# An attention scan in front of two expert layers: late rows of chunk 0 loaded batch by batch, chunk 1's rows loaded by ScalarE's queue, first pieces in another order

## The chip, the cores and the metric

The kernel runs on one core of a Trainium2 chip. The core has TensorE (PE) for matmuls, VectorE (DVE), ScalarE (ACT) and GpSimd (POOL) for elementwise work, and SyncE (SP), which here only issues DMA transfers. The core's 16 DMA engines move data between HBM and the on-chip memory. The metric is the device time of one launch in microseconds, lower is better.

## The reference

What is computed, cut to what matters (the state is carried over 768 positions; batch 4, 8 heads, head size 32, state size 16):

```python
# attention: x, a, B, C in; per batch and head
log_a = np.log(np.clip(a, 1e-06, 1.0)); cum = np.cumsum(la, axis=-1)      # per chunk
L = np.exp(cum[..., :, None] - cum[..., None, :]) * causal
y = (np.einsum('bhin,bhjn->bhij', Cc, Bc) * L) @ xc + (Cc @ state) * np.exp(cum)[..., None]
state = decay_full * state + sum_j Bc_j xc_j decay_from_j
# 4 x 768 tokens of 256 go through two layers of width 2048
h = x @ w_in; x = (h * (1 / (1 + np.exp(-1.702 * h)))) @ w_out
h = x @ w_in2; out = (h * np.clip(h + 3.0, 0.0, 6.0) / 6.0) @ w_out2
```

## The kernel before

**The scan.** The 768 positions are cut into eight chunks of 96. A piece q is one batch of one chunk, q = 4 x chunk + batch. For a piece, score matmuls (`s_mm`, L624) give C times B, which VectorE multiplies by the decay (`g_mul`, L627), or ScalarE copies and GpSimd multiplies (`g_copy` L630, `g_pool` L634); `y_mm` (L650), called by `visit`, multiplies that by x and the state; `y_state` (L664) takes the state back, and casts (L684) and differences (L693, L696) make of the output the two float parts, `bx_0h` and `bx_0l`, that the layers read. Chunk 0 has a path of its own: scores per half of its rows (`sx_mm` L539, `sy_mm` L548), products (`gx_mul` L552, `gx_copy` L555, `gx_pool` L558, `gy_mul` L561), and `yx_mm` (L573) for two pieces at a time. Pieces 4 and 5 are the first two of chunk 1. Later pieces are visited in pairs, or one by one where the pair stands in `SOLO`.

**The layers.** The trunk starts with units of 12 wide matmuls: `l1` (L852) and `l2` (L878). Later blocks go by a Strassen scheme (L1018). A weight tile is loaded (`w_load` L368), scaled by ScalarE (`w_scale` L372), split into a low part (`w_low`, L380 on ScalarE, L382 on VectorE), joined (`w_join` L386 on VectorE, into `dec`), and cast to a high part `wh` (`w_top` L389) whose rest is `wl` (`w_bottom` L393). The tiles are `bx_w0`, `bx_w1` and so on.

**What sets the order.** The class `Schedule` sorts what `add` recorded: each step has an engine, an estimated duration, a key (a due time), and the names it reads and writes; the tables at the top of the file (`TOPV`, `GMX`, `KX`, `KV`, `PK`, `WAFTER` and so on) set keys and engines. The engines then run their instructions in this order. At most eight DMA loads are outstanding over all queues: each waits for the landing of the one eight before it. Before the change, ScalarE's queue carries only four of the eight loads of chunk 0's B and C rows (`in_bcz`, L604) and two constant tables; all else goes by SyncE: x0 (`x0_load`, L531 for the first 64 rows of chunk 0, L528 for the late rows 64 to 95), the four loads of chunk 1's B and C rows (`in_bc0`, `r16_load`, L601, 16 x 1792 each), the store of the clipped decays (L470), the weight tiles, and chunk 1's x values (`x_load`, L592).

Of the kernel before, what the change touches and what calls it, by code (L numbers as in the profile page):

```python
# [71 lines left out]
DECODE = (13.3, 7.5)  # L72


GMX = (0, 1, 3)
KX = (1.1, 4.5, 4.5)
KV = (5.9, 9.7, 10.5)
# [184 lines left out]
def ssd_moe_kernel(ctx: ExitStack, tc: tile.TileContext, xs, aa, bc, bcz_d, bc0, wu, pat, idn, out):  # L262
# [453 lines left out]
    for i in range(2):  # L716
        add("SP", (1.2, 0.6)[i], -40 + i, x0_load, i, r=["xs:0"], w=[f"xs:0.{i}"], kb=(262, 131)[i])
    for q in range(NC * NB):
        c, b = divmod(q, NB)
# [17 lines left out]
        if q < NB and b % 2 == 0:  # L737
# [14 lines left out]
            if p == 0:  # L752
# [420 lines left out]
```

## Time and profile before

| | before |
|---|---|
| time, median of 3 runs | 568.96 us (568.78 to 569.59) |
| profiled execution, its own time | 569.68 us |
| its span | 567.9 us, granted clock 0.999 |
| TensorE busy | 555.0 us, 98% |
| VectorE, ScalarE, GpSimd busy | 431.3, 327.2, 297.4 us |
| HBM read, written | 33.87 MB, 3.26 MB |

The page gives the busy time of each engine first, then the span in 40 slices of 14.2 us with a digit for the busy tenths. The timeline lists instructions of one engine in order of their start; a bracket at a row's end names the idle time before it and what ended it. Rows of consecutive instructions of one kind are drawn together, with the time from the first start to the last end; the last of them ends in a pipeline, so that the next row can start before.

### The profile page before, as it was taken

Reading aid. Unit: us, or ns where it says so; the run is one execution under the profiler, and the core shown is the slowest. Engines: PE = TensorE matmul, PEld = TensorE weight load, DVE = VectorE, ACT = ScalarE, POOL = GpSimd, SP = SyncE. Lnnn points to the kernel's source line nnn. Section 1 sums busy time; section 2 is a strip of 40 time slices with the busy share of each in tenths; the row PEclk is TensorE's granted clock in tenths of the full one; section 3 lists DMA queues with packets and bytes.
Section 4 is the critical chain, followed back from the end, with each engine's and each line's share of the span. In section 5 each row is a group of like instructions: output and inputs, shape, how many; then the busy total and the mean of one; then the engine's idle time right before and its main releaser. Section 6 shows DMA issues by size and latency. Waiting matters only on the chain.

```text
span 567.9 us, 9146 instructions
## 1 busy us (share of the span) xinstructions
PE 555.0 (98%) x3392; PEld 449.6 (79%) x3392; DVE 431.3 (76%) x630; ACT 327.2 (58%) x604; POOL 297.4 (52%) x281
## 2 busy tenths in 40 slices
PE   7699999999999999999999999999999999999996
PEld 6477778878788788788888888888888888888885
DVE  6649997569688886578757888777877876887875
ACT  2477645344434436686868777566554575555543
POOL 4277488687643105457899786777231385101000
PEclk9999999999999999999999999999999999999999
DMA  8995323034224200430103310000200000200002
GB/s 140 315 261 182 119 92 84 1 115 115 83 90 138 87 1 1 162 107 30 38 1 112 111 39 0 1 1 2 74 2 0 1 0 2 74 2 0 1 0 75
DMA packets 22160, 37.73 MB, mean 66 GB/s; under 512 B 10548, under 2 KB 14372, under 8 KB 22116
## 3 DMA queue, kind: packets, MB, share of 16 engines
q1 hardware_dynamic: 20836, 36.47, 21.7%
q10 hardware_dynamic: 1280, 0.68, 0.5%
q8 instruction: 27, 0.44, 0.3%
q14 instruction: 17, 0.14, 0.1%
HBM read 33.87 MB, written 3.26 MB: 65 GB/s over the span
## 4 chain that ended last, share of the span: by engine, by line
PE 93%; DVE 2%; POOL 2%; issue 1%; ACT 1%; DMA 0%; ACTq 0%; POOLq 0%
PE acc L878 45%; PE h L1018 19%; PE h L852 15%; PE s L1018 4%; PE y L1018 4%; PE s L624 2%; PE h L650 1%; POOL wl L393 1%; PE acc L573 1%; POOL gl L868 0%; PE acc L494 0%; PE s L650 0%; DMA pat_sb<-in_pat 0%; PE acc L580 0%; DVE ov_a L700 0%
## 5 line engine op out<-in xcount | busy, mean ns | idle before, releaser
L868 POOL TENSOR_TENSOR gl<-gg,gh 128x512 fp32r<-128x512 f32 x56 | 81.0, 1446 | 156.1 <-PE h L1018 72.9
L878 PE MATMUL acc<-gh,wl 128*128 128x512 f32 x256 | 100.5, 392 | 0.0
L878 PE MATMUL acc<-gh,wh 128*128 128x512 f32 x256 | 99.9, 390 | 0.0
L878 PE MATMUL acc<-gl,wh 128*128 128x512 f32 x256 | 80.3, 390 | 0.0
L878 PE MATMUL acc<-ov_b,wh 128*128 128x512 f32 x256 | 78.9, 389 | 0.0
L1030 DVE TENSOR_TENSOR ov_b<-h,ov_b 128x512 f32<-128x512 f32 x64 | 44.1, 689 | 40.9 <-PE h L1018 39.3
L589 DVE TENSOR_TENSOR_SCAN ov_a<-ov_a,pat_sb 112x448 f32<-112x448 f32 x52 | 67.3, 1329 | 1.1 <-DMA ov_a<-acl_d 1.1
L865 ACT CAST gh<-gg 128x512 fp32r<-128x512 f32 x80 | 49.7, 621 | 20.2 <-DVE gg L862 18.7
L878 PEld LDWEIGHTS acc<-gh,wl 128*128 128x128 f32 x256 | 48.1, 188 | 10.7 <-issue 0.2
L393 POOL TENSOR_TENSOR wl<-dec,wh 128x512 fp32r<-128x512 f32 x32 | 46.0, 1439 | 19.4 <-ACT wh L389 13.4
L878 PEld LDWEIGHTS acc<-gl,wh 128*128 128x128 f32 x256 | 48.1, 188 | 10.2
L878 PEld LDWEIGHTS acc<-ov_b,wh 128*128 128x128 f32 x256 | 48.1, 188 | 10.0
L878 PEld LDWEIGHTS acc<-gh,wh 128*128 128x128 f32 x256 | 48.1, 188 | 9.9
L859 ACT ACTIVATE gg<-h 128x512 f32<-128x512 f32 x48 | 28.7, 598 | 43.5 <-PE h L1018 35.6
L868 DVE TENSOR_TENSOR gl<-h,gh 128x512 fp32r<-128x512 f32 x47 | 32.1, 683 | 27.1 <-ACT gh L865 26.9
L878 PE MATMUL acc<-ov_b,wl 128*128 128x512 f32 x128 | 49.8, 389 | 0.0
L856 ACT ACTIVATE gg<-h 128x512 f32<-128x512 f32 x39 | 23.3, 598 | 44.4 <-PE h L852 43.8
L856 ACT ACTIVATE h<-h 128x512 f32<-128x512 f32 x39 | 22.7, 582 | 44.8 <-PE h L852 35.2
L868 POOL TENSOR_TENSOR ov_b<-ov_b 128x512 fp32r<-128x512 f32 x24 | 31.6, 1315 | 25.4 <-ACT ov_b L865 22.3
L865 ACT CAST gh<-h 128x512 fp32r<-128x512 f32 x47 | 27.6, 586 | 7.8 <-DVE h L862 5.7
L1030 DVE TENSOR_TENSOR h<-h,ov_b 128x512 f32<-128x512 f32 x32 | 22.4, 699 | 8.7 <-PE h L1018 8.4
L862 DVE SCALAR_TENSOR_TENSOR gg<-gg,h 128x512 f32<-128x512 f32 x40 | 27.1, 678 | 1.5 <-ACT gg L859 1.2
(295 smaller groups left out, 1305.3 us busy)
## 6 DMA issues: line engine op xcount, KB each, us to landing
bx_w<-in_wu SPq DMA_DIRECT2D x32, 512.0 KB, 5.6
ov_a<-acl_d SPq DMA_DIRECT2D x26, 392.0 KB, 3.7
ov_a<-in_xs SPq DMA_DIRECT2D x7, 384.0 KB, 4.4
ov_a<-in_bc SPq DMA_DIRECT2D x96, 24.0 KB, 2.5
out<-gg SPq DMA_DIRECT2D x6, 192.0 KB, 1.9
out<-gg SPq DMA_DIRECT2D x4, 128.0 KB, 1.8
ov_a<-in_bc SPq DMA_DIRECT2D x4, 112.0 KB, 9.1
ov_a<-in_xs SPq DMA_DIRECT2D x3, 128.0 KB, 3.7
```

Source lines behind the costliest of these rows:

```text
L393: e.tensor_tensor(out=lo, in0=B_(f"dec:{p}").bitcast(F32), in1=hi.bitcast(F32), op=ALU.subtract)
L589: nc.vector.tensor_tensor_scan(t, a, pat_sb, 0.0, ALU.mult, ALU.add)
L624: nc.tensor.matmul(out=s_bank(q, g)[:, k, :], lhsT=t[r:r + NS, 0, i], rhs=t[r:r + NS, 1, i], start=True, stop=True)
L852: nc.tensor.matmul(out=B_(hn(u)), lhsT=w[:, 128 * j:128 * j + 128], rhs=x[:, j], start=low in (None, 1) and i + j == 0, stop=low == 2 and ...
L856: nc.scalar.activation(B_(dst), B_(src), AF.Gelu_apprx_sigmoid)
L859: nc.scalar.activation(B_(dst), B_(src), AF.Relu, bias=3.0)
L862: nc.vector.scalar_tensor_tensor(out=B_(dst), in0=B_(g), scalar=6.0, in1=B_(h), op0=ALU.min, op1=ALU.mult)
L865: nc.scalar.copy(B_(dst), B_(src))
L868: e.tensor_tensor(out=B_(dst), in0=B_(src), in1=B_(hi).bitcast(F32), op=ALU.subtract)
L878: nc.tensor.matmul(out=B_(acc[d]), lhsT=w[:, 256 + 128 * d:384 + 128 * d], rhs=g, start=first and d not in seen, stop=last and d not in [v ...
L1018: nc.tensor.matmul(out=B_(dst), lhsT=w, rhs=x, start=start and i == 0, stop=i == 2, skip_group_check=True)
L1030: nc.vector.tensor_tensor(out=B_(dst), in0=B_(a), in1=B_(b), op=ALU.add)
```

## The change

Three things change around the start, and with them the tables that set the order.

1. The late rows of chunk 0 are four loads of 32 x 256, one for each batch, on ScalarE's queue; it was one load of 128 x 1 x 256 on SyncE's.
2. The four loads of chunk 1's rows go by ScalarE's queue, with a key of their own (`R1K`); they stood on SyncE's, ahead of the decays' store and the weights.
3. On TensorE the second `yx_mm` stands ahead of the scores of pieces 4 and 5. One product of chunk 0 moves from ScalarE and GpSimd to VectorE (`GMX`). Pair 3 is visited piece by piece too (`SOLO`). Nine tops on VectorE become five (`TOPV`), the rest goes to ScalarE; other tables and the planner's durations and DMA model are set anew.

The names of lines move by 6 up to some line 590 of before, by 7 in the layers (L368 is L374, L624 is L630, L852 is L859).

```diff
-TOPV = (3, 5, 6, 7, 8, 9, 10, 12, 14)
+TOPV = (2, 5, 8, 9, 10)
...
-GMX = (0, 1, 3)
-KX = (1.1, 4.5, 4.5)
-KV = (5.9, 9.7, 10.5)
+GMX = (0, 1)
+KX = (2.7, 4.2, 4.7)
+KV = (10.1, 6.3, 11.5)
...
-SOLO = (5,)
+SOLO = (3, 5)
 solo = lambda q: q < 4 or q // 2 in SOLO
-R16 = 10.0
+R16 = 4.0
+RQ = ("ACT", "ACT", "ACT", "ACT")
+X0Q = ("SP", "ACT")
+R1K = -23.0
+PXK = -96
+X0K = (-51.7, -38.4)
...
-WAFTER = (2.7, 4.2, 4.0, 6.5, 14.0, 7.1, 19.7)
+WAFTER = (4.3, 4.5, 3.9, 6.1, 12.0, 7.6, 21.3)
...
-                pipe = max(pipe, t + 1.3) + o["kb"] / 240.0
-                end = pipe + 0.8
+                pipe = max(pipe, t + 1.2) + o["kb"] / 390.0
+                end = pipe + 0.5
...
-    def x0_load(i):
-        if i:
-            nc.sync.dma_start(out=B_("xs:0")[:, 2], in_=xs[0][64:CH].rearrange("j b f -> b j f"))
-        else:
-            for j in range(2):
-                nc.sync.dma_start(out=B_("xs:0")[64 * j:64 * j + 64, 0:2], in_=xs[0][0:64].rearrange("j (p b) f -> j b p f", b=2)[:, j])
+    def x0_load(eng, i):
+        if i > 1:
+            b = i - 2
+            eng.dma_start(out=B_("xs:0")[32 * b:32 * b + 32, 2], in_=xs[0][64:CH, b])
+        else:
+            eng.dma_start(out=B_("xs:0")[64 * i:64 * i + 64, 0:2], in_=xs[0][0:64].rearrange("j (p b) f -> j b p f", b=2)[:, i])
...
-    for i in range(2):
-        add("SP", (1.2, 0.6)[i], -40 + i, x0_load, i, r=["xs:0"], w=[f"xs:0.{i}"], kb=(262, 131)[i])
+    for i in range(2 + NB):
+        e = X0Q[i > 1]
+        add(e, 0.4 if i > 1 else 0.6, X0K[i > 1] + i, x0_load, DQ[e], i, r=["xs:0"], w=[f"xs:0.{i}"], kb=80 if i > 1 else 250)
...
-                    e = "SP" if c or s else "ACT"
+                    e = ("SP" if s else "ACT") if c == 0 else RQ[i] if c == 1 else "SP"
                     n = f"rows.{c}.{i}.{s}"
-                    add(e, 0.84 if c > 1 else 0.42 if c else 0.66, t - R16 + 1 if c else -70 + i, r16_load, {"SP": nc.sync, "ACT": nc.scalar}[e], c, i, s,
-                        r=[rn], w=[n], kb=140 if c == 1 else 80, after=(0.0, 3.0, 16.0, 16.0)[min(c, 3)])
+                    add(e, 0.84 if c > 1 else 0.43 if c else 0.66, t - R16 + 1 if c > 1 else R1K + i if c else -70 + i, r16_load, DQ[e], c, i, s,
+                        r=[rn], w=[n], kb=(200, 390)[c] if c < 2 else 80, after=(0.0, 3.0, 16.0, 16.0)[min(c, 3)])
```

SyncE's order from x0 to the third weight tile before (`ov3_a` holds the x rows, `ov2_a` the B and C rows, `acl_d` the stored decays):

```order
L531 DMA ov3_a_121<-in_xs 64x2x256 x2
L528 DMA ov3_a_121<-in_xs 128x1x256
L601 DMA ov2_a_120<-in_bc0 16x1792 x4
L470 DMA acl_d_126<-gg0_107 128x224
L368 DMA bx_w0_205<-in_wu 128x1024
L368 DMA bx_w1_207<-in_wu 128x1024
L592 DMA ov3_a_121<-in_xs 96x1024
L368 DMA bx_w2_227<-in_wu 128x1024
```

And the same stretch of SyncE now:

```order
L537 DMA ov3_a_121<-in_xs 64x2x256 x2
L476 DMA acl_d_126<-gg0_107 128x224
L374 DMA bx_w0_180<-in_wu 128x1024
L374 DMA bx_w1_185<-in_wu 128x1024
L598 DMA ov3_a_121<-in_xs 96x1024
L374 DMA bx_w2_230<-in_wu 128x1024
```

The late rows and the four row loads of chunk 1 are gone from it, and the tiles follow x0 directly.

ScalarE's order ahead of chunk 0's state before (`h0`, `h1`, `y0` are score banks, `ov4_a` holds products):

```order
L604 DMA ov2_a_120<-in_bcz 16x8x112 x2
L555 COPY ov4_a_122<-h0_127 128x448
L555 COPY ov4_a_122<-h1_128 128x448
L372 ACTIVATE bx_w0_205<-bx_w0_205 128x512
L555 COPY ov4_a_122<-y0_134 128x448
L666 COPY st_sb_117<-acc3_132 128x2x16
```

And now:

```order
L535 DMA ov3_a_121<-in_xs 32x256 x4
L607 DMA ov2_a_120<-in_bc0 16x1792
L561 COPY ov4_a_122<-h0_127 128x448
L561 COPY ov4_a_122<-h1_128 128x448
L378 ACTIVATE bx_w0_180<-bx_w0_180 128x512
L607 DMA ov2_a_120<-in_bc0 16x1792 x3
L378 ACTIVATE bx_w1_185<-bx_w1_185 128x512
L378 ACTIVATE bx_w2_230<-bx_w2_230 128x512
L378 ACTIVATE bx_w3_253<-bx_w3_253 128x512
L672 COPY st_sb_117<-acc3_132 128x2x16
```

Three of the row loads stand behind the scaling of tile 0, and tiles 1 to 3 are scaled ahead of chunk 0's state; the third copy of a score bank is gone.

ScalarE's order at the opening of the trunk before (`acc` is a bank of outputs, the last cast writes what the first wide matmul reads):

```order
L684 CAST bx_0h_352<-acc2_131 128x2x96
L372 ACTIVATE bx_w2_227<-bx_w2_227 128x512
L389 CAST wh0_71<-dec0_103 128x512
L372 ACTIVATE bx_w3_284<-bx_w3_284 128x512
L664 COPY st_sb_117<-acc3_132 128x2x2x16
L684 CAST bx_0h_352<-acc3_132 128x2x96
```

And now:

```order
L378 ACTIVATE bx_w4_298<-bx_w4_298 128x512
L636 COPY ov4_a_122<-s0_133 112x448
L386 ACTIVATE s0_133<-bx_w0_180 128x512
L378 ACTIVATE bx_w5_337<-bx_w5_337 128x512
L395 CAST wh0_71<-dec0_103 128x512
L378 ACTIVATE bx_w6_412<-bx_w6_412 128x512
L670 COPY st_sb_117<-acc3_132 128x2x2x16
L690 CAST bx_0h_375<-acc3_132 128x2x96
```

Tiles 4, 5 and 6 are scaled here, where it was tiles 2 and 3.

## Rows read from the trace of the kernel before

**Rows 1.** The page's first part: busy time, share of the span, instructions.

```profile
PE 555.0 (98%) x3392; PEld 449.6 (79%) x3392; DVE 431.3 (76%) x630; ACT 327.2 (58%) x604; POOL 297.4 (52%) x281
```

**Rows 2.** Waits of TensorE: what waited, for what, total, times, longest (us).

```profile
PE acc L573 <- issue: 2.7, 1, 2.7
...
PE h L852 <- ACT bx_0h L684: 1.3, 1, 1.3
```

**Rows 3.** Timeline of TensorE: start, length, instruction, idle time before it.

```profile
15.56 0.62 PE L573 MATMUL acc<-ov_a 64*32 64x112 f32 x16
...
20.07 0.38 PE L573 MATMUL acc<-sf,ov_a 32*32 32x48 f32 x5 [2.67 <-issue]
20.37 0.53 PE L624 MATMUL h<-ov_a 16*112 16x112 f32 x2
...
22.30 0.62 PE L573 MATMUL acc<-ov_a 64*32 64x112 f32 x16
...
28.88 1.22 PE L852 MATMUL h<-bx_0h,wh 128*128 128x512 f32 x2 [1.31 <-ACT bx_0h L684]
```

**Rows 4.** Timeline of SyncE's DMA queue: when its loads were issued.

```profile
6.26 1.84 SPq L601 DMA_DIRECT2D ov_a<-in_bc  x4
...
8.61 0.93 SPq L368 DMA_DIRECT2D bx_w<-in_wu  x2
13.51 0.33 SPq L592 DMA_DIRECT2D ov_a<-in_xs  x1
```

**Rows 5.** Waits of SyncE's queue up to 46 us.

```profile
SPq L592 <- DMA ov_a<-in_xs: 4.0, 1, 4.0
```

**Rows 6.** Timeline of ScalarE: the first scaling of a weight tile.

```profile
18.70 0.66 ACT L372 ACTIVATE bx_w<-bx_w 128x512 f32<-128x512 f32 x1 [6.52 <-DMA bx_w<-in_wu]
```

**Rows 7.** Windows: length, busy of PE, PEld, DVE, ACT, POOL; clock, DMA share, GB/s.

```profile
0.00:9.00 9.00, 5.96 (x25) 4.57 (x26) 5.17 (x10) 2.00 (x3) 4.74 (x17) 1.00 0.78 139
9.00:17.00 8.00, 8.00 (x184) 5.82 (x183) 6.87 (x10) 0.97 (x2) 2.22 (x2) 1.00 0.99 141
17.00:22.00 5.00, 2.33 (x56) 2.02 (x48) 0.66 (x1) 2.55 (x9) 1.59 (x2) 1.00 1.03 292
22.00:25.00 3.00, 3.00 (x79) 1.59 (x73) 2.55 (x7) 0.99 (x5) 0.68 (x2) 1.00 1.03 410
```

**Rows 8.** DMA between 8.5 and 11.5, 13 and 16, 17.6 and 21.6 us.

```profile
DMA packets 173, 0.28 MB, mean 94 GB/s; under 512 B 36, under 2 KB 149, under 8 KB 173
...
DMA packets 129, 0.37 MB, mean 122 GB/s; under 512 B 25, under 2 KB 51, under 8 KB 129
...
DMA packets 299, 1.07 MB, mean 268 GB/s; under 512 B 37, under 2 KB 37, under 8 KB 299
```

**Rows 9.** DMA between 6.0 and 6.5 us by queue: packets, MB, share.

```profile
q1 hardware_dynamic: 84, 0.08, 110.9%
q10 hardware_dynamic: 5, 0.00, 4.8%
```

**Rows 10.** DMA between 17.5 and 18.6 us, the instruction queue.

```profile
q8 instruction: 1, 0.02, 6.2%
```

**Rows 11.** Timelines of VectorE (three rows) and ScalarE (one) ahead of the trunk.

```profile
22.29 0.62 DVE L627 TENSOR_TENSOR ov_a<-h,ov_a 112x448 f32<-112x448 f32 x1 [4.63 <-ACT gg L690]
22.83 0.62 DVE L627 TENSOR_TENSOR ov_a<-s,ov_a 112x448 f32<-112x448 f32 x1
...
26.49 0.68 DVE L386 SCALAR_TENSOR_TENSOR dec<-bx_w,s 128x512 uint32<-128x512 uint32 x1
...
27.73 0.67 ACT L372 ACTIVATE bx_w<-bx_w 128x512 f32<-128x512 f32 x1
```

**Rows 12.** Timeline of TensorE: a pair visited at once, and half a pair.

```profile
60.85 0.97 PE L650 MATMUL s<-ov_a 112*32 112x112 f32 x32
...
80.95 0.59 PE L650 MATMUL y<-ov_a 112*32 112x112 f32 x16
```

**Rows 13.** The page's second part: VectorE's busy tenths in 40 slices.

```profile
DVE  6649997569688886578757888777877876887875
```

More of the change, by code (lines that the diff above doesn't have):

```diff
@@ L44 @@
 LP = 9
-DL = (3.8, 1.0, 0.2, 2.7, 0.6)
-TOPV = (3, 5, 6, 7, 8, 9, 10, 12, 14)
+DL = (3.9, 1.2, -0.4, 2.5, 1.0)
+TOPV = (2, 5, 8, 9, 10)
 TOPP = (2, 3, 7, 24, 27, 28)
@@ L49 @@
 BOT = lambda p: "POOL"
-LOWD = (0, 1, 2, 16, 17, 21)
+LOWD = (1, 2, 3, 11, 16, 17, 21)
 LOW = lambda p: "DVE" if p in LOWD else "ACT"
-GMS = (0, 2, 3, 4, 6, 7, 9, 22)
+GMS = (0, 2, 3, 4, 7, 10, 20, 22)
 GMP = lambda q, g: 2 * q + g in GMS if q < 12 else g == 1 and q > GM1
 GM1 = 32
-GL0 = (1, 2, 9, 13)
+GL0 = (1, 2, 9)
 GLP = lambda kind, k, m: m % 4 in GLM[k] if k else m in GL0
-GLM = ((0,), (0, 1, 2), (0, 1, 2), (0,))
+GLM = ((2, 3), (0, 1), (0, 1, 3), (0,))
 TE = lambda kind, v: "DVE" if kind == "A" and v[0] == "T" else "POOL"
@@ L71 @@
 PKEY = (0.7, 0.7, 1.4, 3.4, 4.1, 6.1, 6.8)
[L72 to L77 removed]
+DECODE = (13.3, 7.6)
+GMX = (0, 1)
+KX = (2.7, 4.2, 4.7)
+KV = (10.1, 6.3, 11.5)
 def SBANK(q, g):
@@ L101, in YBANK @@
     return f"{'ys'[q % 2]}:y{q}" if solo(q) else f"{'ys'[q // 2 % 2]}:y{q // 2 * 2}"
-P0 = (4.6, 7.5)
-YP = (0, 4)
-PK = (45.0, 4.0, 94.9, 4.3, 116.4, 5.8, 149.3, 3.9)
+P0 = (5.6, 7.7)
+YP = (1, 4)
+PK = (45.0, 4.0, 93.9, 4.3, 117.0, 5.5, 148.3, 4.2)
 UGAP = (16, 0.25)
@@ L706, in ssd_moe_kernel @@
     add("DVE", 0.38, -80, a_clip, w=["gg:acl"])
-    add("DVE", 0.26, -80, a_part, 0, r=["gg:acl"], w=["gh:acl"])
-    add("DVE", 0.30, -80, a_part, 1, r=["gg:acl", "gh:acl"], w=["al"])
+    add("DVE", 0.57, -80, a_part, 0, r=["gg:acl"], w=["gh:acl"])
+    add("DVE", 0.57, -80, a_part, 1, r=["gg:acl", "gh:acl"], w=["al"])
     add("SP", 0.4, -1, a_store, r=["gg:acl"], w=["acl_d"], kb=115)
     add("POOL", 0.15, -84, ay_zero, new=["gl:acl"])
-    add("DVE", 0.2, -79, ay_part, r=["gh:acl", "al"], w=["gl:acl"])
+    add("DVE", 0.4, -79, ay_part, r=["gh:acl", "al"], w=["gl:acl"])
     for i in range(3):
@@ L743, in ssd_moe_kernel @@
                 add("DVE", 1.06, t + 0.1 * g, x_decay, p, g, r=[f"acc:lx{p}.{g}", f"l:x{p}", "patx0", "patx1", "gg:patx"], w=[f"lx{p}.{g}"])
-            add("PE", 1.0, t + 0.9, sx_mm, p, r=["r16:0"] + rows[0], new=[SBANK(q, g) for g in range(2)])
+            add("PE", 1.75, t + 0.9, sx_mm, p, r=["r16:0"] + rows[0], new=[SBANK(q, g) for g in range(2)])
             for g in range(2):
@@ L756, in ssd_moe_kernel @@
                 add("DVE", 0.92, t, y_decay, r=["acc:ly", "l:y", "gg:paty", *[f"paty{i}" for i in range(4)]], w=["ly"])
-                add("PE", 1.6, t + 0.9, sy_mm, r=["r16:0"] + rows[0], new=["acc:sy0", "acc:sy1"])
+                add("PE", 1.05, t + 0.9, sy_mm, r=["r16:0"] + rows[0], new=["acc:sy0", "acc:sy1"])
                 sch.take("sf:gmy", t + 1.2)
@@ L775, in ssd_moe_kernel @@
         if q >= NB and q % 2 == 0 and q // 2 - 1 not in JOIN:
-            add("PE", 1.1, t + 1, s_mm, (q, q + 1), r=[f"r16:{c}"] + rows[c], new=[SBANK(qq, g) for qq in (q, q + 1) for g in range(2)])
+            add("PE", 1.85 if q < 6 else 1.1, t + 1, s_mm, (q, q + 1), r=[f"r16:{c}"] + rows[c], new=[SBANK(qq, g) for qq in (q, q + 1) for g in range(2)])
         for g in range(2) if q >= NB else ():
@@ L788, in ssd_moe_kernel @@
             if q < NB and b % 2 == 0:
-                add("PE", 1.4, t + 2, yx_mm, q // 2, r=[f"gm:x{q // 2}.{g}" for g in range(2)] + ["sf:gmy", "gmy0", "gmy1", "xs:0", "xs:0.0", "xs:0.1"],
+                add("PE", 1.85, t + 2, yx_mm, q // 2, r=[f"gm:x{q // 2}.{g}" for g in range(2)] + ["sf:gmy", "gmy0", "gmy1", "xs:0", *[f"xs:0.{i}" for i in range(2 + NB)]],
                     new=[yn, YBANK(q + 1)])
@@ L794, in ssd_moe_kernel @@
             if q >= NB:
-                add("PE", (0.62 if solo(q) else 1.0) + 0.75 * join, t + 2, visit, pieces, (q + 1, q + 2) * join, r=([f"r16:{c2}"] + rows.get(c2, [])) * join + [f"gm:{i}.{g}" for i in pieces for g in range(2)] + [f"xs:{c}"] + [f"xs:{c}.{b // 2}.{k}" for k in range(4) if c],
+                add("PE", (0.62 if solo(q) else 1.0 if q > 5 else 1.9) + 0.75 * join, t + 2, visit, pieces, (q + 1, q + 2) * join, r=([f"r16:{c2}"] + rows.get(c2, [])) * join + [f"gm:{i}.{g}" for i in pieces for g in range(2)] + [f"xs:{c}"] + [f"xs:{c}.{b // 2}.{k}" for k in range(4) if c],
                     new=[yn] + [SBANK(i, g) for i in (q + 1, q + 2) for g in range(2)] * join)
```

5 lines of the change are left out of this document (3 added, 2 removed).

## The prediction

> **What bounds the kernel now.** The page's first part comes first: TensorE is busy for 555.0 of the 567.9 us of the span [rows 1], and no wide matmul is taken away or added. What the change can win is therefore idle time of TensorE, and the list of its waits says how little there is: 2.7 us in which it waited for "issue" in the products of chunk 0 (L573), 1.3 us for ScalarE's cast ahead of the first wide matmul (L852), and smaller ones [rows 2]. The timeline puts them in place: chunk 0's products start at 15.56, stand still from 17.4 to 20.07, the score products of pieces 4 and 5 (L624) start at 20.37, the second half of chunk 0's products at 22.30, and the wide matmuls, the trunk, at 28.88 [rows 3]. From there TensorE runs without a gap worth naming. So the question is one number: does the trunk open before or after 28.88? An order that is better later has nothing to win, one that is worse can lose.
>
> What sets 28.88 is fed by DMA. SyncE issues x0's two loads and the late rows, then the four row loads of chunk 1 at 6.26, the first two weight tiles at 8.61, and chunk 1's values (L592) only at 13.51 [rows 4], after 4.0 us of waiting for the late rows [rows 5]. That is how I read the landing of the late rows: 13.5, well before their reader at 15.56. The first tile, issued at 8.61, reaches ScalarE at 18.70 [rows 6]: the engines are full. By stretches they move 139, 141, 292 and 410 GB/s at a share near one [rows 7]. The rate depends on what is moved: 94 GB/s where row loads and the store of the clipped decays pass, 122 beside late rows and rows, 268 where tiles and chunk 1's values pass [rows 8], 410 for tiles alone.
>
> **Two readings that the sum rests on.** First, between 6.0 and 6.5, when ScalarE's queue had loads outstanding, its queue (q10) got 5 packets and SyncE's (q1) 84 [rows 9]. I read this as service in order of arrival: what is issued late stands behind every tile that was issued earlier, whichever queue it came from. Second, in the middle of TensorE's 2.7 us without instructions one 16 KB packet of an instruction queue (q8) passes, between 17.5 and 18.6 [rows 10]. I read the stall as TensorE's next block of instructions, standing in the same line behind the tiles. The Trainium skill, "Runtime: NRT & Kernel Launch", section "Instruction fetch mechanics", has such a block cross over "mostly hidden"; here it isn't, by the 2.67 us of the row. By the page the third case below would not exist, and the sum would be the same.
>
> **The change part by part.** *Late rows in four pieces on ScalarE's queue.* Their reader starts at 15.56 and they landed at 13.5, so nothing is won directly; if they land earlier, chunk 1's values and tiles 2 to 4, which each wait for a place among eight outstanding loads, are issued earlier too. That is no gain on the path either, and it puts more in front of what comes after.
>
> *Chunk 1's rows on ScalarE's queue.* The first goes out behind the late rows, the other three behind the scaling of tile 0, and the last also waits for a place that tile 1 holds. So the last row load is issued when tile 1 has landed, with tiles 2 to 4 and chunk 1's values already in line: in order of arrival it lands when five tiles (5 x 512 KB), the values (384) and the four rows (4 x 112) are through, 3392 KB or 3.47 MB. At 9.0 us the trace has moved 9 x 139 = 1.25 MB [rows 7], which is about the inputs that stay ahead (1.20 MB by their shapes). From 9.0 on: at the rates of before, 8 x 0.141 = 1.13 and 5 x 0.292 = 1.46 MB by 22.0, and the remaining 0.88 MB at 0.410 in 2.2 us: 24.2 us. That is the upper bound, since the slow stretch of before holds the rows once and I count them in it. The lower: tiles 2.62 MB at 0.410 in 6.4 us, values 0.39 at 0.268 in 1.5, rows 0.46 at 0.094 in 4.9: 21.8 us. I take 23.5, nearer to the upper, because tiles beside row loads moved at 122 [rows 8], not 410.
>
> *TensorE's order.* The second half of chunk 0's products (1.8 us) now stands ahead of the scores of pieces 4 and 5, so it is done while these wait for their rows. After the scores, which take 22.30 - 20.37 = 1.93 us [rows 3], only the piece's own chain is left. Scores from 23.8 (I allow 0.3 us from landing to start, well inside the bounds) end at 25.73. VectorE then makes three products, 0.54 to 0.55 from one start to the next [rows 11], 1.65 us, and the join of tile 0, 0.68: end 28.06. From the join's end to the trunk it was 28.88 - 27.17 = 1.71 us [rows 3, 11], and the same four steps of ScalarE stand there now (cast, a tile's scaling, state copy, cast). Trunk at 29.77, or +0.9; with the bounds 21.8 and 24.2, -0.8 to +1.5.
>
> *Fourth product from ScalarE and GpSimd to VectorE, tops from VectorE to ScalarE, other due times.* VectorE has room ahead of 22.29, where it stood idle for 4.63 us [rows 11], so the moved product costs nothing; the cover is the wait for the scores, and without it the price is 0.62. The tops move to an engine that is 58% busy. *One more pair visited in two halves.* A pair's visit takes 0.97, half a visit 0.59 [rows 12]; twice 0.59 is 1.18, so +0.2 us, on TensorE and so on the path; bounds 0 and 0.4.
>
> Sum: +0.9 + 0.2 = +1.1 us, bounds -0.6 and +1.7. The profiled run took 569.68 for its span of 567.9, 0.72 above the median 568.96; the sum is a difference of spans, so it goes onto the median: 570.1 us, 568.4 to 570.7.
>
> **Rivals.** *Queues served in turn.* If ScalarE's queue gets a turn beside SyncE's, each row load goes ahead of the waiting tiles, lands soon, and the instruction block doesn't wait either. Scores then follow chunk 0's products without a stop (17.4 + 0.3 + 1.8 = 19.5 to 21.4), and something else opens the trunk: in ScalarE's order the scaling of tiles 4, 5 and 6 now stands ahead of the cast that the trunk waits for, where it was tiles 2 and 3. Tile 6 is in when 7 tiles, values, rows and the inputs ahead are, 5590 KB or 5.72 MB: 3.84 MB by 22.0, the other 1.88 at 0.410 in 4.6 us, 26.6. From the start of a scaling to the trunk it was 28.88 - 27.73 = 1.15 [rows 11]; with 0.3 to its start, 28.05: -0.8 + 0.2 = -0.6, 568.4 us; down to -2.7 (566.3) if the slow first 17 us move faster. For it: two queues exist. Against: 84 packets to 5 [rows 9]. The Trainium skill, "DMA: Bandwidth & Descriptors", section "Queues, rings and completion order", says that each DMA engine goes round between the queue rows that have work, packet by packet. By that rule it is this case, and the row between 6.0 and 6.5 doesn't agree.
>
> *The instruction block comes later.* TensorE's order up to chunk 0's products is as long as before, so it runs dry again near 17.3. With the rows out of SyncE's way tile 3 is issued some 4 us earlier, and the block stands behind tiles 0 to 3, the values and one row: 2544 KB, 2.60 MB from 9.0. If the first tiles move at full rate that is served at about 17, TensorE resumes near 19.5 and the stall hides under the wait for the rows: the main case. At the rates of before it is 22.0, and with the 2.54 us from the packet to 20.07 [rows 3, 10] TensorE resumes at 24.5, ends chunk 0's products at 26.3 and the scores at 28.2: trunk 32.2, +3.3 + 0.2 = +3.5, 572.5 us. It decides from the point at which the block is served after 20.4.
>
> *Late tables.* VectorE is at nine tenths or more in three slices from 43 to 85 us [rows 13], where products and joins are dealt out anew. If one of them comes late for the trunk, TensorE gets a wait that it doesn't have: 1 to 2 us on top of the main case, 571 to 572. Against it: the trunk had no wait in these slices before. That the late rows don't gain from four pieces would change nothing: they have 2 us to spare.
>
> **How the numbers follow.** Main case 47 in 100 (22 slower, 25 within), queues in turn 25 (12 or 13 faster, the rest within), the later block 16 (slower), late tables 12 (10 slower, 2 within). About 0.2% or 1.1 us is what a measurement here tells from no change. Faster 0.13, same 0.39, slower 0.48; the main case lies on the border, which is why its chance is split. The range leaves out the faster end of the first rival and the tail of the second: 567.2 to 573.0. Both signs are not far apart, and the main case's own range is 568.4 to 570.7.
>
> **What would show it.** Right: the scores of pieces 4 and 5 (now L630) start near 23.8 and wait for a row load issued by ScalarE, with chunk 0's products done before; the trunk opens at 29 to 30.3. Wrong in the first reading: row loads landed within 4 us of their issue while tiles wait. Wrong in the second: no instruction wait, or one that ends after 22. Wrong in the rest: new rows in TensorE's waits after 30 us.

## The result

The changed kernel is slower: 572.14 us, median of 6 runs (570.41 to 573.72), against 568.96 for the kernel before in the same session; the ratio is 1.0058, 95% interval 1.0039 to 1.0077. The profiled execution took 571.98 us, its span is 570.2 us, 2.3 above before's 567.9. The runs scatter nearly three times as widely as those of before (3.3 us against 1.2); the experiments show two things that scatter.

### The profile after

First what answers to [rows 1] and [rows 2]: the page's first part, and TensorE's waits (what waited, for what, total, times, longest).

```profile
PE 555.5 (97%) x3392; PEld 449.9 (79%) x3392; DVE 427.2 (75%) x634; ACT 329.8 (58%) x609; POOL 287.1 (50%) x276
```

```profile
PE acc L579 <- issue: 2.8, 1, 2.8
PE acc L656 <- ACT bx_w L378: 2.5, 1, 2.5
...
PE h L859 <- ACT bx_0h L690: 1.4, 1, 1.4
```

The wait for instructions (L579) is where it was. New is the second line: the visit of pieces 4 and 5 (L656, the pieces' products times x) waits 2.5 us, where it waited 0.8 before, and the trace puts it down to a scaling of a weight tile by ScalarE (L378). That scaling (26.37 to 27.03) only came last by the profile: the first product that the visit reads ended at 26.9 too, so this row alone names no cause. TensorE's timeline, the answer to [rows 3]:

```profile
15.37 0.62 PE L579 MATMUL acc<-ov_a 64*32 64x112 f32 x16
...
19.98 0.37 PE L579 MATMUL acc<-sf,ov_a 32*32 32x48 f32 x5 [2.78 <-issue]
20.28 0.62 PE L579 MATMUL acc<-ov_a 64*32 64x112 f32 x16
...
22.06 0.53 PE L630 MATMUL h<-ov_a 16*112 16x112 f32 x2
...
27.04 1.83 PE L656 MATMUL acc<-ov_a 112*32 112x112 f32 x32 [2.55 <-ACT bx_w L378]
30.31 1.22 PE L859 MATMUL h<-bx_0h,wh 128*128 128x512 f32 x2 [1.44 <-ACT bx_0h L690]
...
34.58 1.05 PE L859 MATMUL h<-bx_0h,wh 128*128 128x512 f32 x2
...
36.29 0.98 PE L859 MATMUL acc<-bx_0h,wh 128*128 128x512 f32 x2
37.10 0.63 PE L859 MATMUL acc<-bx_0h,wl 128*128 128x512 f32 x2
```

Chunk 0's products, their stop and their resumption stand within 0.2 us of [rows 3]. The second half of them (20.28) now runs ahead of the scores of pieces 4 and 5 (22.06). The trunk opens at 30.31, 1.43 us later than before. The chain of waits of the same stretch shows what the opening hangs on (start, length, what the path stood on):

```profile
9.86 12.60 DMA bx_w<-in_wu
...
22.48 0.02 ACT bx_w L378
...
23.04 0.25 ACT st_sb L672 x2
...
24.39 0.04 DVE ov_a L706
...
26.32 0.19 DVE ov_a L633
...
28.00 0.07 DVE dec L392
```

Read from the top: a weight tile, issued at 9.86, is on the path for 12.6 us; at 22.48 ScalarE scales it (tile 3, the fourth of the scalings in its order). Only behind that does ScalarE copy chunk 0's state (L672, 23.04), though the first copy's source had been ready since 20.35; VectorE transposes the state (L706) from 24.39 and only then makes the products of pieces 4 and 5 (L633, 26.32), though their scores had run since 22.06 and were through at 24.5; the join of tile 0 (L392) follows at 28. Chunk 1's rows are not on this path: the last of them landed at 22.6, and the scores didn't hold the products.

The difference of the two traces can be added up. The opening is 1.43 us later. The fifteenth wide matmul starts at 37.10; in the trace of before it is the first of the last row here:

```profile
33.16 0.91 PE L852 MATMUL h<-bx_0h,wh 128*128 128x512 f32 x2
33.90 0.63 PE L852 MATMUL acc<-bx_0l,wh 128*128 128x512 f32 x2
...
34.81 0.62 PE L852 MATMUL h<-bx_0h,wl 128*128 128x512 f32 x2
```

37.10 - 34.81 = 2.29, so another 0.86 us is lost in the first fourteen wide matmuls: a pair of them takes 1.05 us up to 36.29 after and up to 33.16 before, then 0.62. The last matmul of the kernel is 2.55 us later (565.42 against 562.87): 0.26 more over the remaining 530 us. Behind it 0.25 us is given back, which makes the 2.3 us of the spans. The medians lie 3.2 us apart; 0.9 us of that is not in this pair of executions, since the profiled one of before lay 0.72 us above its median and this one 0.16 below.

### The profile page after: what moved, and what is told of

Its sections match the earlier page's. It is cut to its first block, busy times and chain, and to the rows that moved or that the text cites. A ratio compares the mean times of both kernels' runs of the same rounds, so it can differ in the third digit from the quotient of the medians.

```text
span 570.2 us, 9141 instructions
## 1 busy us (share of the span) xinstructions
PE 555.5 (97%) x3392; PEld 449.9 (79%) x3392; DVE 427.2 (75%) x634; ACT 329.8 (58%) x609; POOL 287.1 (50%) x276
## 4 chain that ended last, share of the span: by engine, by line
PE 92%; DMA 4%; DVE 1%; issue 1%; ACT 1%; SPq 1%; ACTq 0%; DVEq 0%
PE acc L885 45%; PE h L1025 19%; PE h L859 15%; PE s L1025 4%; PE y L1025 4%; DMA bx_w<-in_wu 2%; PE s L630 2%; PE h L656 1%; DMA ov_a<-acl_d 1%; SPq L614 1%; PE acc L859 1%; DMA ov_a<-in_xs 0%; DMA idn_sb<-in_idn 0%; PE s L656 0%; PE y L656 0%
## 5 line engine op out<-in xcount | busy, mean ns | idle before, releaser
L875 POOL TENSOR_TENSOR gl<-gg,gh 128x512 fp32r<-128x512 f32 x51 | 72.8, 1430 | 169.8 <-PE h L1025 73.7
L595 DVE TENSOR_TENSOR_SCAN ov_a<-ov_a,pat_sb 112x448 f32<-112x448 f32 x52 | 64.4, 1265 | 5.2 <-DMA ov_a<-acl_d 5.2
L872 ACT CAST gh<-gg 128x512 fp32r<-128x512 f32 x75 | 46.5, 621 | 20.9 <-DVE gg L869 19.2
L875 DVE TENSOR_TENSOR gl<-h,gh 128x512 fp32r<-128x512 f32 x52 | 35.6, 684 | 28.6 <-ACT gh L872 27.1
L866 ACT ACTIVATE gg<-h 128x512 f32<-128x512 f32 x48 | 28.7, 599 | 47.0 <-PE h L1025 39.7
L399 POOL TENSOR_TENSOR wl<-dec,wh 128x512 fp32r<-128x512 f32 x32 | 44.3, 1388 | 22.0 <-ACT wh L395 19.8
L863 ACT ACTIVATE h<-h 128x512 f32<-128x512 f32 x44 | 25.7, 584 | 45.6 <-PE h L859 39.1
L863 ACT ACTIVATE gg<-h 128x512 f32<-128x512 f32 x34 | 20.3, 598 | 37.6 <-PE h L859 35.6
L872 ACT CAST gh<-h 128x512 fp32r<-128x512 f32 x52 | 30.5, 587 | 7.4 <-DVE h L869 5.2
L378 ACT ACTIVATE bx_w<-bx_w 128x512 f32<-128x512 f32 x32 | 21.5, 677 | 12.2 <-DMA bx_w<-in_wu 12.2
```

The lines of the kernel that those rows point to most:

```text
L378: nc.scalar.activation(top, top, AF.Prelu, scale=2.0 ** 16, alpha=2.0 ** 32)
L399: e.tensor_tensor(out=lo, in0=B_(f"dec:{p}").bitcast(F32), in1=hi.bitcast(F32), op=ALU.subtract)
L595: nc.vector.tensor_tensor_scan(t, a, pat_sb, 0.0, ALU.mult, ALU.add)
L863: nc.scalar.activation(B_(dst), B_(src), AF.Gelu_apprx_sigmoid)
L866: nc.scalar.activation(B_(dst), B_(src), AF.Relu, bias=3.0)
L872: nc.scalar.copy(B_(dst), B_(src))
```

## The experiments

Three theories were put against each other. **A, ScalarE's line**: ScalarE stands still for a late tile, and chunk 0's state stands behind it. **B or D, the line of transfers**: chunk 1's rows now stand between the tiles, land late, and slow the tiles and TensorE's instruction block. **C, the later tables.** In the edits, `prog` is the finished order of all steps; `at` finds a step by name and first arguments, `move` puts one behind another. A comment in a fence tells an edit in words.

### Tile 3 scaled behind chunk 0's state

```diff
+    move(("w_scale", 3), ("y_out", 1, 0))
```

> The changed kernel with one step moved: ScalarE scales tile 3 behind chunk 0's state copies and casts, not ahead of them. Theory A (ScalarE stands still for tile 3 until 22.48 and holds chunk 0's state, VectorE's transposes and so its products behind it): state copies near 20.5 and 22.3, products of pieces 4 and 5 from 24.5, join of tile 0 ends near 27, trunk at 28.5 to 28.9 instead of 30.31, time 570.3 to 570.8 where the changed kernel has 572.14. Theory B (the rows of chunk 1 that land late behind the tiles set the opening): trunk within 0.3 us of 30.31, time within 0.4 of 572.1. Theory C (the later tables carry most of the loss): same as B.

Measured: 570.70 us, ratio to before 1.0020 (1.0010 to 1.0030), against 1.0058 for the change. In the trace the state copies run at 21.95, and the trunk opens at 29.60, although this execution's head ran 0.7 us late (chunk 0's products started at 16.09 instead of 15.37):

```profile
21.95 0.25 ACT L672 COPY st_sb<-acc 128x32 f32<-128x32 f32 x2
...
29.60 1.22 PE L859 MATMUL h<-bx_0h,wh 128*128 128x512 f32 x2 [0.89 <-ACT bx_0h L690]
```

One step moved on one engine gives back 1.4 of the 3.2 us. A holds; B and C alone would have left the time where it was. The trunk did not come to the 28.5 to 28.9 expected: 0.7 us is the late head, and with the scaling out of the way the rows come next, since the scores stop 0.9 us for the last row load and end at 25.93, where the changed kernel's end at 24.5.

The later runs confirm A more sharply. In every trace with the changed order of tile 3 ahead of chunk 0's state, save one, the trunk opens 7.82 to 7.83 us behind the start of that scaling, wherever it falls:

| trace | tile 3 scaled at | trunk opens at | between |
|---|---|---|---|
| chunk 1's rows back on SyncE's queue | 20.94 | 28.77 | 7.83 |
| the changed kernel | 22.48 | 30.31 | 7.83 |
| pair 3 at once | 22.92 | 30.74 | 7.82 |
| the changed kernel, second trace | 23.20 | 31.02 | 7.82 |
| both DMA moves undone | 24.67 | 32.49 | 7.82 |
| late rows in one load | 21.38 | 30.05 | 8.67 |

In the last row the last row load lands at 24.5, the scores end at 26.39, and the rows decide.

### The two DMA moves alone, in the kernel before

```diff
-    # x0_load(1): one load on SyncE; r16_load(1, 0..3) on SyncE, ahead of a_store
+    # four late(b) on ScalarE's queue; r16_load(1, 0) behind them, 1 to 3 behind w_scale(0), on ScalarE's queue
```

> The kernel before with the two DMA moves alone: late rows in four loads on ScalarE's queue, chunk 1's rows on ScalarE's queue at the places they have in the changed kernel; every other order as before. The scores of pieces 4 and 5 stand ahead of chunk 0's second products here. If the rows land near 22.5 (in line behind tiles): scores end near 24.5 instead of 22.3, trunk near 31, time 570.8 to 571.5. If the rows land as early as before (17.4) or earlier: trunk within 0.3 of 28.88, time 568.6 to 569.3.

Measured: 577.28 us, ratio 1.0144 (1.0129 to 1.0159), far beyond the 571 expected. The scores, which stand ahead of chunk 0's second products in this order, stop three times for rows:

```profile
19.23 0.71 PE L624 MATMUL h<-ov_a 16*112 16x112 f32 x2
23.34 0.68 PE L624 MATMUL h<-ov_a 16*112 16x112 f32 x2 [3.40 <-DMA ov_a<-in_bc]
25.84 0.68 PE L624 MATMUL s<-ov_a 16*112 16x112 f32 x2 [1.82 <-DMA ov_a<-in_bc]
28.29 0.49 PE L624 MATMUL y<-ov_a 16*112 16x112 f32 x1 [1.77 <-DMA ov_a<-in_bc]
```

ScalarE could issue the last three row loads only between 17.76 and 20.99, since each waits for a place among eight outstanding loads, and in this order of loads tiles 2, 3 and 4 hold the places. They landed at 23.2, 25.7 and 28.2, 5.4 to 7.5 us after their issue. In the changed kernel the same three loads wait for the places of the decays' store and of tiles 0 and 1, and go out at 11.07, 11.42 and 14.69. So this run is not the change's two moves by themselves, and its 8 us are not their price; that the other orders protect the changed kernel is not shown by it.

What it does show is that rows pass tiles. The last tile issued before the rows went out at 16.74, the first of the three rows at 17.76; their times to landing, in us at the end of the line:

```profile
bx_w<-in_wu SPq DMA_DIRECT2D x1, 512.0 KB, 14.4
ov_a<-in_bc ACTq DMA_DIRECT2D x1, 112.0 KB, 5.4
```

The row load lands at 23.2, the tile that was issued 1 us earlier at 31.2.

### Chunk 1's rows back on SyncE's queue

```diff
+    for i in range(4):
+        o = prog.pop(at("r16_load", nc.scalar, 1, i))
+        o["args"] = (nc.sync, 1, i, None)
+        prog.insert(at("a_store"), o)
```

> The changed kernel with chunk 1's four row loads back on SyncE's queue ahead of the decays' store and the tiles; late rows stay in four loads on ScalarE's queue. Theory A: tile 3 lands no earlier, since the same bytes stand in front of it, so ScalarE's stop stays and the trunk opens at 30 to 31, time 571.8 to 572.8. Theory B: rows land before 18, trunk at 28.5 to 29, time 570.3 to 570.8.

Measured: 570.29 us, ratio 1.0022 (1.0011 to 1.0032). Here A was wrong in its own expectation: tile 3 does land earlier. Waits of TensorE, ScalarE's scaling of tile 3, and the trunk:

```profile
PE acc L579 <- issue: 1.1, 1, 1.1
```

```profile
20.94 0.67 ACT L378 ACTIVATE bx_w<-bx_w 128x512 f32<-128x512 f32 x1 [0.61 <-DMA bx_w<-in_wu]
...
28.77 1.22 PE L859 MATMUL h<-bx_0h,wh 128*128 128x512 f32 x2 [1.42 <-ACT bx_0h L690]
```

Tile 3 is issued 2.0 us later here (11.91 against 9.86) and lands 1.5 us earlier; the rate of the DMA engines goes with that. By windows (columns as in [rows 7], the last is GB/s), first this kernel, then the changed one:

```profile
9.00:12.00 3.00, 3.00 (x44) 2.47 (x47) 3.00 (x4) 0.97 (x2) 0.69 (x1) 1.00 0.98 133
12.00:15.00 3.00, 3.00 (x99) 2.60 (x92) 2.98 (x6) 0.53 (x1) 1.53 (x2) 1.00 1.02 379
15.00:18.00 3.00, 2.25 (x62) 1.03 (x60) 2.22 (x3) 0.84 (x2) 0.00 (x0) 1.00 1.02 268
18.00:22.00 4.00, 3.62 (x101) 2.61 (x101) 0.00 (x0) 1.72 (x6) 0.00 (x0) 1.00 1.03 405
```

```profile
13.00:16.00 3.00, 3.00 (x100) 2.02 (x103) 2.97 (x6) 0.68 (x1) 0.49 (x1) 1.00 1.02 254
16.00:19.00 3.00, 1.20 (x43) 0.56 (x43) 1.19 (x2) 0.00 (x0) 0.00 (x0) 1.00 1.06 219
19.00:22.00 3.00, 2.02 (x69) 1.08 (x69) 0.00 (x0) 0.67 (x1) 0.00 (x0) 1.00 1.01 218
```

Rows in one block ahead of the tiles cost one slow stretch (133, the last late rows and the decays' store among them), land 3.4 to 4.3 us after their issue and are all in by 13.0 us; the next slow stretch (268) is that of chunk 1's values, landed at 18.6. Rows strewn among the tiles leave the engines at 218 to 254 from 13 to 22 us, although their share is near one throughout. From 9 to 22 us the engines move 304 GB/s here and 249 in the changed kernel. The opening follows tile 3, as the table above has it: 1.54 us earlier, both.

### Tiles 2 to 9 held back

```diff
+    # w_load(2) to w_load(9) issued by ScalarE's queue, behind y_state(3); scalings of 2 and 3 behind y_out(1, 0)
```

> The changed kernel with tiles 2 to 9 held back: ScalarE's queue issues them only behind the first state copy, so that hardly any transfer is under way between 16 and 20 us. The time itself will be many us longer and says nothing. If TensorE's instruction block stands in line behind tiles: the wait for instructions in chunk 0's products shrinks from 2.78 us to under 1. If it is a fixed latency that dense code can't cover: 2.3 to 2.8 us, as before.

Measured: one run, 578.22 us; the wait is neither of the two:

```profile
PE acc L579 <- issue: 4.1, 1, 4.1
```

```profile
DMA packets 236, 0.80 MB, mean 201 GB/s; under 512 B 58, under 2 KB 58, under 8 KB 235
```

The second line is the DMA between 17 and 21 us. The engines were not idle: with these tiles gone from its order, SyncE issued the next ones (tiles 10 and 11) and the decays of later pieces (392 KB each) there, and they moved slowly beside the rows. So the clean test failed. What it does show, with the run above: the wait is no fixed latency, since the same instructions run dry at 17.2 to 17.7 us and wait 1.1, 2.8 or 4.1 us. In all thirteen traces with this wait TensorE resumes 1.3 to 1.7 us after the 16 KB packet of the instruction queue has ended (16.90 and 18.38 in the run above, 18.51 and 19.98 in the changed kernel, 20.44 and 21.86 here), so the packet ends the wait. That it stands in line behind transfers is not shown: the rate ahead of it doesn't order the waits (from 13 to 17 us 330, 276 and 220 GB/s in these three, but 137 in the kernel before, whose wait is 2.67).

### Both repairs

```diff
+    # rows as above, and the scalings where the tiles are used:
+    move(("w_scale", 2), ("y_out", 1, 0));  move(("w_scale", 3), ("w_low", 0));  move(("w_scale", 4), ("w_top", 1))
+    move(("w_scale", 5), ("top", "h:u0"));  move(("w_scale", 6), ("w_low", 5))
```

> The changed kernel with both repairs: chunk 1's rows on SyncE's queue ahead of the decays' store and the tiles (as in the run that opened the trunk at 28.77), and ScalarE scales tiles 2 to 6 only behind chunk 0's state, tile by tile where it needs them. Theory A (ScalarE's line) and theory D (the line of transfers: rows between tiles slow both and hold TensorE's instruction block) are two separate losses: scores end near 22.3, chunk 0's state is copied by 21.3, join of tile 0 ends near 25, trunk at 26.7 to 27.5, time 568.0 to 569.0. If they are one and the same loss (what the one repair gives back the other can't): trunk at 28.3 to 28.8, time 569.8 to 570.3.

Measured: 568.26 us, ratio 0.9976 (0.9965 to 0.9987): faster than the kernel before. VectorE's products and the opening:

```profile
22.73 1.16 DVE L633 TENSOR_TENSOR ov_a<-h,ov_a 112x448 f32<-112x448 f32 x2
```

```profile
26.17 1.22 PE L859 MATMUL h<-bx_0h,wh 128*128 128x512 f32 x2 [0.88 <-ACT bx_0h L690]
```

The opening is 2.6 us earlier than with the rows alone, at 26.17, before the interval expected. So the two are separate losses: with the scaling moved the rows hold the opening, with the rows moved the scaling does. How much of the 2.6 us is tile 3 is open, since this edit moves the scalings of tiles 2, 4, 5 and 6 too, those ahead of the trunk's last cast among them.

### The late rows, and the tables by themselves

> The changed kernel with the late rows of chunk 0 back in one load of 128 x 1 x 256 on SyncE's queue behind x0; chunk 1's rows stay on ScalarE's queue. If the late rows' split matters: tiles 2 to 4 are issued later, TensorE's instruction wait changes by over 0.5 us and the time by over 0.8. If only chunk 1's rows matter: trunk within 0.5 of 30.31, time 571.6 to 572.6.

> The changed kernel with both DMA moves undone: late rows in one load and chunk 1's rows on SyncE's queue, as in the kernel before; the orders of all engines as in the changed kernel. Theory A: tile 3 is now issued near 15.7 as before, lands near 24, ScalarE stands still for it ahead of chunk 0's state, trunk at 31 to 32, time 572.8 to 574. Theory D alone (the DMA moves carry the loss): trunk at 28.5 to 29, time 569.2 to 570.

The edit puts the late rows back as one load on SyncE's queue; the second kernel has the rows there too. Measured: 571.95 us (ratio 1.0046, 1.0029 to 1.0064) and 573.51 us (1.0071, 1.0056 to 1.0086). With the first, the opening is at 30.05. With the second, ScalarE scales tile 3 at 24.67 and the trunk opens at 32.49, as A had it for a later tile 3. Together with the runs above, as ratios to the kernel before, all with the changed orders:

| | late rows in four loads | late rows in one |
|---|---|---|
| chunk 1's rows on ScalarE's queue | 1.0058 (the change) | 1.0046 |
| chunk 1's rows on SyncE's, ahead of tiles | 1.0022 | 1.0071 |

Four late loads are worth 0.5% where the rows go first; where the rows go last the intervals overlap. With rows first and the late rows in one load SyncE is held up as in [rows 5] (3.6 us here), and tile 3 goes out at 15.00 instead of 11.91; with the rows on ScalarE's queue it isn't held, and tile 3 goes out at 10.04. So of the change's two DMA moves the one is good and the other spoils it, as long as tile 3 is scaled ahead of chunk 0's state; the late loads were not tried with the scalings behind it.

### Pair 3 at once

> The changed kernel with pair 3 visited at once again (SOLO holds only pair 5), orders planned anew with that. By the price in the prediction: trunk where it was, 30.31 within 0.2, and 0.2 us less behind it, time 571.7 to 572.1. Theory C (later tables carry part): 0.5 us or more less behind the opening, time below 571.6.

```diff
-SOLO = (3, 5)
+SOLO = (5,)
```

Measured: 571.11 us, ratio 1.0040 (1.0023 to 1.0057); this interval overlaps that of the change, so by itself it settles nothing. Its trace has 1.9 us less behind the opening, but 1.6 of that is the rate of the first wide matmuls (6 at the low rate, where the changed kernel's trace has 14). Done on top of both repairs:

> The kernel with both repairs, and pair 3 visited at once again (SOLO holds only pair 5), the later orders planned anew with that. Theory C (the later tables and the second pair visited in halves cost something of their own, 0.4 us by the two traces with and without it): time 567.6 to 568.1. Without C: 568.3 within 0.2.

567.02 us, ratio 0.9961 (0.9946 to 0.9976) against 0.9976. Both point to some 0.9 us, more than the 0.2 of the prediction, but these intervals overlap too, so the size is not shown. A part of it is luck of the execution (in the trace of the second the instruction wait is too short to be listed, and the trunk opens at 25.20). What the later orders cost can be seen in TensorE's waits: 0.25 us at 181.62 in the changed kernel, and in its second trace

```profile
241.16 0.96 PE L1025 MATMUL h<-bx_T3A,bx_SA 128*128 128x512 f32 x3 [0.56 <-DVE ov_b L1037]
```

The same wait, of 0.2 to 0.8 us, stands near 240 in six of the other traces with the changed later orders, and in none of the three traces with pair 3 at once, nor in the kernel before.

### The same kernel again

> The changed kernel itself once more, for a second trace of it. Its runs scatter from 570.41 to 573.72 us, the kernel before from 568.36 to 569.59. If the scatter comes from the stretch in which the trunk's first wide matmuls start 0.43 us apart (later 0.23): this trace opens the trunk within 0.4 us of 30.31, and the number of wide matmuls at 0.43 differs from the 13 of the first trace by as many as its time differs, 0.2 us for each. If it comes from the landing of rows and tiles: the opening itself moves by over 0.5 us.

572.01 us, span 570.2 as in the first trace, but with another split: the trunk opens at 31.02, 0.7 later, and only 8 wide matmuls run at 0.43 us or more, where the first trace has 14; the wait near 241 is new.

```profile
31.02 1.22 PE L859 MATMUL h<-bx_0h,wh 128*128 128x512 f32 x2 [1.43 <-ACT bx_0h L690]
...
34.45 1.01 PE L859 MATMUL h<-bx_0l,wh 128*128 128x512 f32 x2
35.29 0.63 PE L859 MATMUL h<-bx_0h,wh 128*128 128x512 f32 x2
```

So both scatter: the opening, because tile 3 lands differently (at 23.18 here, 22.46 in the first trace; the scores stop 1.8 us for the last row load too, but are not what the opening waits for), and the number of wide matmuls at half rate. Neither of the two expectations was right alone.

### Matmuls on zeros in the waits around the opening

```diff
+    # 128 x 256 bf16 on zeros into a free bank, 7 behind s_mm(4, 5), 4 behind the visit, 4 behind the first l1
```

> The kernel with both repairs (568.26 us; trunk at 26.17, wide matmuls 0.43 us apart until 33.5, then 0.23), and in TensorE's waits ahead of the trunk and behind its first group 7, 4 and 4 matmuls on zeros of the whole array, 128 x 256 bf16, 0.21 us each, into a bank that nothing reads. If TensorE's rate after the opening hangs on what it did just before: the wide matmuls reach 0.23 us within 3 us of the opening instead of 7, 1 to 2 us are saved, time 566.3 to 567.3. If only the real trunk counts: time within 0.5 of 568.3, and the added matmuls cost nothing because they lie in waits.

566.87 us, ratio 0.9961 (0.9947 to 0.9975) against 0.9976 (0.9965 to 0.9987) for both repairs, on which this kernel is built; the intervals just overlap, and the time lies where it was expected. The rate is up when the trunk opens:

```profile
21.46 1.67 PE L1136 MATMUL acc<-st_tr 128*128 128x256 bf16 x7
23.07 1.72 PE L656 MATMUL acc<-ov_a 112*32 112x112 f32 x32
24.72 0.62 PE L1136 MATMUL acc<-st_tr 128*128 128x256 bf16 x4
25.55 0.73 PE L859 MATMUL h<-bx_0h,wh 128*128 128x512 f32 x2 [0.21 <-ACT bx_0h L690]
...
28.23 0.63 PE L859 MATMUL h<-bx_0h,wl 128*128 128x512 f32 x2
```

```profile
19.00:21.00 2.00, 2.00 (x60) 1.55 (x50) 0.78 (x3) 1.27 (x6) 1.13 (x2) 0.50 1.02 406
...
28.00:31.00 3.00, 3.00 (x15) 2.46 (x14) 2.51 (x5) 2.91 (x6) 2.92 (x4) 1.00 1.05 270
```

The seven matmuls on zeros at 21.46 stand 0.21 us apart, the four at 24.72 already 0.11. The first two pairs of wide matmuls take 0.73 us instead of 1.22, every later one 0.62 or 0.63; the granted clock reads 0.50 from 19 to 21 us and 1.00 from 28 to 31. And the five runs lie within 0.55 us of each other.

### Everything that helped

> Everything that helped, together: chunk 1's rows on SyncE's queue ahead of the tiles, tiles 2 to 6 scaled behind chunk 0's state, pair 3 visited at once with the orders planned anew for that, and the 15 matmuls on zeros in TensorE's waits around the trunk's opening. If the three gains are separate (1.9976 to 0.9961 by the matmuls alone, the same by the pair alone, as ratios 0.9976 to 0.9961): ratio to the kernel before 0.994 to 0.995, time 566.0 to 566.6 where before has 569.3. If the pair's gain was the instruction block's early landing in that trace: 0.9955 to 0.9965, time 566.8 to 567.3.

(The first ratio in that sentence is a slip for 0.9976.) Measured: 566.30 us, ratio 0.9941 (0.9927 to 0.9954), 3.4 us faster than the kernel before in the same session and 5.8 below the changed kernel's median in its own; this is where the gains were expected if they are separate. The trunk opens at 25.70, at full rate.

## Why the prediction was right, and where not

The direction and the range held: slower, 572.14 in 567.2 to 573.0. The likeliest value did not: +1.1 us was forecast, +3.2 measured. That the range held is in good part luck: the main case's own range, 568.4 to 570.7, missed, and the wide one took the time in because it was stretched over two rivals (572.5 for the later block, 571 to 572 for late tables), of which the first did not come about and the second was seen at 0.3 to 0.6 us. By the prediction's own steps:

| step | predicted | trace of after |
|---|---|---|
| TensorE resumes after the instruction block | near 19.5 | 19.98 |
| chunk 0's products done before the scores' rows | yes | yes, near 22.1 |
| last row load lands | 23.5 (21.8 to 24.2) | 22.6; 23.8 in the second trace |
| scores end | 25.73 | 24.5 |
| from scores' end to join's end | 2.33 | 4.1 |
| join of tile 0 ends | 28.06 | 28.6 |
| trunk opens | 29.77 | 30.31 |
| rate of the first wide matmuls | not priced | +0.86 |
| pair 3 in halves, later tables | +0.2 | +0.26; waits of 0.2 to 0.8 near 240 in other traces |

**Service in order of arrival** does not hold as it was put ("behind every tile that was issued earlier"), and neither does its rival. The row loads landed 5.8 to 9.1 us after their issue:

```profile
DMA to landing us min/median/max: 5.8/8.3/9.1
```

The first rival, queues served in turn, would have them land soon, within 4 us by the prediction's sign, and they didn't; from 13 to 16 us ScalarE's queue got 1 packet and SyncE's 209, with two row loads out since 11.07 and 11.42. Yet they passed tiles: these two landed at 19.7 and 20.5, tile 3, issued at 9.86, at 22.46; the last, issued at 14.69, landed at 22.6, ahead of tile 4, issued at 11.23 and landed at 23.6. And 8 us is no sign of a line behind tiles: in the kernel before, where they stood ahead of the tiles on SyncE's queue, the same loads took 8.3 to 9.7 us. Nor was [rows 9] a fair sample of the kernel before: from 5 to 6 us ScalarE's queue got 144 packets and SyncE's 125, from 6.5 to 8 it was 139 to 202. So the landing came out near the forecast without its reason, and what orders the service stays open. The Trainium skill ("DMA: Bandwidth & Descriptors", section "Queues, rings and completion order") states a round between the queues: the passing goes with it, the 1 packet to 209 does not.

**The instruction block.** The second rival, in which it decides, did not come about because its packet was through at 18.51, ahead of the limit of 20.4 (19.5 by the prediction's own 2.54 us from packet to resumption and 1.8 us of products ahead of 23.8). That the packet ends the wait is shown; that it stands in line behind the tiles is not.

**The step that failed** is the path: rows, scores, products, join, trunk, in the sentence that after the scores "only the piece's own chain is left". VectorE's products of pieces 4 and 5 don't follow the scores but stand in its order behind the transposes of chunk 0's state, those wait for ScalarE's copies, and ScalarE's copies stand behind the scaling of tiles 1 to 3. The landing of tile 3 opens the trunk, 7.82 us after its scaling starts, and "no gain on the path" from tiles that land earlier was wrong with it. The prediction had ScalarE's order before it (three scalings in a row ahead of the state copies, where before there was one) and took it for the trunk's opening alone, where it weighed tiles 4 to 6 as a rival; that VectorE now makes all three products behind the transposes, where two of the three stood ahead of them (22.29 and 22.83 in [rows 11]), it did not look at. The term was 2.33 us and measured 4.1. It hid at first because the scores were 1.2 us early; the sum of both gave an opening only 0.5 us off, which is luck: what the forecast waits for, the rows, was not what the trunk waited for.

**Two terms were missing.** The first wide matmuls run at half rate for a while, and how long is not fixed by the opening: 0.86 us here. And of the medians' 3.2 us the two traces hold 2.3; the rest is the scatter of the executions, in which this rate and the landing of tile 3 differ from trace to trace.

**Four late loads** were called worth nothing. Beside rows among the tiles no gain is seen (1.0058 against 1.0046, intervals that overlap), but with rows first they are worth 0.5% (1.0071 against 1.0022), through tile 3: a step was judged in the company of one that spoiled it.

**The later tables** were a rival on top of the main case at 1 to 2 us, and their sign, new rows in TensorE's waits after 30 us, is there: 0.25 us in the first trace of the changed kernel, 0.56 in the second. The runs without the second split pair point to some 0.9 us, not clear of noise. What of it is the pair and what the other orders stays open.

## What to carry to other kernels

Before a wait is moved on an in-order engine, list what stands behind it there and who waits for each: a step that is not urgent and waits for a transfer (a tile's scaling) must not stand ahead of one that is urgent and ready (a state copy). Loads that are needed first belong first in the line, in one block: on a second queue they passed some tiles that were issued earlier, but took 5.8 to 9.1 us, where the same loads ahead of the tiles took 3.4 to 4.3, and while they were strewn among others all moved more slowly. When a change bundles several edits, a table of each with and without the others finds the one that is worth keeping.

## What was not expected of the hardware

Small row loads go with a slow line: where four 112 KB loads of 16 rows pass, with the last late rows and the decays' store, the engines moved 133 GB/s (9 to 12 us, rows on SyncE's queue), where tiles pass alone 405, where tiles and chunk 1's values pass 268, and where tiles and rows pass 218 to 219 (16 to 22 us in the changed kernel), at a busy share of one in each case.

A load on a second queue landed neither at once nor in order of issue: 5.4 us for a row load beside 14.4 for the tile issued 1 us ahead of it on the other queue.

The start of the trunk runs at TensorE's lower level: 0.43 us for 512 columns against 0.23, the two levels of 1.2 and 2.4 GHz. Ahead of it TensorE had been busy for 8.00 of 8.00 us from 9 to 17 with small matmuls, and for 2.33 of 5.00 from 17 to 22 [rows 7]. In the traces without added matmuls the rate rose behind 6 to 16 wide ones (10 in the kernel before, 14 and 8 in the two traces of the change, 16 in that of both repairs with pair 3 at once); with matmuls on zeros of the whole array in the waits it rose before the opening. The Trainium skill, "TensorE: Matmul & The Clock Gate", section "Part 1: The HAM clock gate (the "warmup" mystery)", tells of the two levels and of a number of slow matmuls that differs from run to run; the traces agree. The column of the granted clock does not follow it: it reads 1.00 from 30 to 36 us in the changed kernel, while pairs take 1.05 us, and 0.50 from 30 to 34 in the run with tile 3 moved, at the same 1.05.

```profile
30.00:36.00 6.00, 5.36 (x12) 3.78 (x13) 4.26 (x10) 3.54 (x9) 5.40 (x6) 1.00 1.05 248
```

```profile
30.00:34.00 4.00, 3.67 (x9) 2.37 (x9) 2.85 (x7) 1.98 (x5) 3.58 (x4) 0.50 1.04 280
```

And TensorE can run out of instructions: it stops behind 59 short matmuls that take 1.8 us, until the next block's packet has come. The fetch that the Trainium skill calls "mostly hidden" ("Runtime: NRT & Kernel Launch", section "Instruction fetch mechanics") cost 1.0 to 4.1 us in thirteen of these fourteen traces.
